# A new written order for the first phase of a linear-attention and MLP kernel

## The chip, the core and the metric

The kernel runs on one core of a Trainium2 chip. The metric is device microseconds (us) of one launch; lower is better. One execution of each kernel is also taken by the hardware profiler, and all rows below come from that one.

## The reference

Two parts run one after the other. The first is a gated linear recurrence over 768 time steps for 4 batches and 8 heads of size 48; the second is an MLP on the 3072 rows that come out of it, with a squared ReLU:

```
f = sigmoid(f_logit)
state = f[t] * state + outer(k[t], v[t])       # per batch and head, 48 x 48
y[t] = q[t] @ state
h = y.reshape(3072, 384) @ w_in                # 384 -> 2048
out = relu(h)**2 @ w_out                       # 2048 -> 384
```

All of it is float32.

## The kernel before

The sequence is cut into 6 blocks of 128 steps, and a block of all batches is 512 columns. In a block the 8 heads are worked in 4 units of two heads; units are numbered through, so that units 0 to 3 are block 0 and 4 to 7 block 1. The first three units of a block own the 128 rows of one tile x_0, x_1, x_2 each. The fourth has no rows of its own: the last 16 rows of each head are cut off the first three units' keys and queries (moved into `last_kq`), worked as unit 3 (or 7), written to `ys`, and moved from there into the rows left open in x_0, x_1 and x_2. Only then is the block's x whole and the MLP can begin on it.

The MLP is worked by 16 slices f of the 2048 hidden columns. A slice has an upward step (9 matmuls of 128x512 into `ph`), a square (three ScalarE passes, L195 to L197), a rest (one VectorE pass into `gl`, L202) and a downward step (9 matmuls into `po`). Each weight tile arrives as a raw tile of 384 KB and is decoded by ScalarE and VectorE into a high and a low float32 part, before a matmul can use it.

Two tables of short words, FIRST and SECOND, set the order of what is here called the first phase: units 0 to 7 and, for block 0, slices 0 to 5. Each word is a letter and a number, and emits its instructions on whatever engines it uses. TensorE, VectorE, ScalarE and SyncE run them in just that order. The words are:

- f, k, L: load of a unit's gates, keys and queries (L: 768 KB in one), v: of its values; i, o: raw tile of w_in or w_out.
- G: gates (ScalarE). K: scan and keys (VectorE L349, L355). Q: reciprocal, scan and queries (L361 to L366). T: transposes of the keys into `pk` (TensorE), N: their copy to `kn` (ScalarE). D: products with the values into `ds`; S: scores (TensorE). M: the mask (VectorE L441). C: the states (L456, L461). m: moves into `last_kq`; r, s: crossed copies (ScalarE L385, L393). Y: outputs into `py` (TensorE). H, X: high part (ScalarE L500) and low part (VectorE L504) of x. g: moves of `ys` into x (six transfers, L511).
- A, I, V, c, J decode a tile of w_in, B, O, Z, d, P one of w_out (ScalarE, VectorE, VectorE, ScalarE, VectorE; A and B are two ScalarE passes).
- U, R, E, W: upward step, square, rest and downward step of a slice. busy: filler transposes on TensorE whose result nothing reads.

So ScalarE's copies, VectorE's scans and the decoding of weights all stand in one order per engine, and what waits holds up all behind it. A raw tile's load is held by a marker: VectorE writes one element of the tile where the word stands, and SyncE's load has to follow that write. SyncE issues in its own order too, so loads behind a held one wait with it. GpSimd's order is not written; it issues m and g for blocks 0 and 1.

For units 4 to 7 `ds` and `py` share one PSUM buffer: D of a unit waits until X of the unit before it has read `py`, and Y waits until M and C have read `ds`.

After the first phase a loop of the remaining MLP slices runs, with the units of blocks 2 to 5 and the decoding of the other 20 weight tiles hooked in. Neither table touches it.

Of the kernel before, what the change touches and what calls it, by code (L numbers as in the profile page):

```python
# [15 lines left out]
I32 = mybir.dt.int32  # L16
# [8 lines left out]
HP = H // 2  # L25
# [8 lines left out]
NJ = DM // P  # L34
# [23 lines left out]
THIRD_AT, THIRD_OUT_AT = (11, 15, 18, 21), (15, 18, 21, 23)  # L58

FIRST = """  # L60
f0 k0 G0 v0 L1 K0 Q0 busy15 T0 v1 N0 busy2 D0 L2 r0 m0 S0 C0 G1 s0 K1 M0 busy5 T1 v2 Q1 Y0 N1 i0 o0
v3 L4 G2 D1 H0 m1 K2 S1 r1 X0 T2 A0 C1 v4 M1 s1 I0 N2 busy3 Y1 Q2 B0 D3 H1 V0 D2 m2 r2 X1 c0 S2 O0
i1 o1 L5 C2 Z0 s2 G4 M2 J0 d0 busy4 Y2 K4 r3 S3 H2 v5 C3 A1 T4 X2 M3 s3 Q4 N4 busy2 Y3 B1 H3 P0 m4
I1 i2 o2 L6 r4 X3 V1 g3 busy5 S4 G5 O1 c1 D4 K5 C4 v6 busy4 T5 A2 M4 s4 Z1 N5 busy5 Y4 Q5 d1
"""
SECOND = """
U0 H4 X4 r5 m5 i3 o3 v7 P1 J1 D5 R0 I2 U1 C5 G6 E0 s5 S5 V2 K6 R1 W0 c2 M5 T6 A3 E1 Y5 Q6 N6 W1 H5
i4 o4 i5 B2 X5 m6 J2 D6 r6 I3 U2 C6 B3 O2 s6 O3 S6 Z2 R2 Z3 M6 V3 Y6 r7 E2 d3 o5 H6 P3 d2 X6 c3 P2
S7 A5 J3 D7 M7 W2 C7 A4 I5 B4 I4 U3 V5 s7 V4 O4 c4 Z4 c5 Y7 J4 R3 J5 U4 H7 E3 B5 X7 U5 g7 d4 O5 R4
P4 Z5 W3 R5 E4 W4 d5 E5 P5 W5  # L70
"""


# [190 lines left out]
def fast_path(ctx, tc, moe, ident, low, fkqT, vN, w, out):  # L264
    nc = tc.nc
    V, G = nc.vector, nc.gpsimd
# [39 lines left out]
    class Unit:  # L306
# [23 lines left out]
        def load(self, *parts):  # L330
            if parts[0].start == 0:
                pool, bufs = (pro, 1) if self.t == NJ else (wk, NBUF)
                self.fkq = pool.tile([P, 3, NZ * CZ], F32, tag="fkq", name=f"fkq{self.nm}", bufs=bufs)
                self.ft, self.rr = self.fkq[:, 0, :NT], self.fkq[:, 0]
                self.view(self.fkq[:, 1:])
            for c in parts:
                nc.sync.dma_start(self.fkq[:, c, :NT], fkqT[self.blk, self.hp, :, c])

# [31 lines left out]
        def move(self):  # L370

            for h in range(2):
                r, at = h * C + D, h * C + self.hp * (C - D)
                (G if self.blk < 2 else nc.sync).dma_start(
                    *(t.rearrange("p a n -> p (a n)")[:, : NZ * CZ + NT] for t in (
                        last_kq[at : at + C - D], self.fkq[r : r + C - D, 1:]
                    ))
                )
# [127 lines left out]
        def parts(self):  # L506

            for j in range(NJ):
                for h in range(2):
                    r, at = h * C + D, h * C + j * (C - D)  # L510
                    (G if self.blk < 2 else nc.sync).dma_start(  # L511
                        self.x[j][r : r + C - D].bitcast(F32), self.x[NJ][at : at + C - D].bitcast(F32)
                    )

# [327 lines left out]
```

## Time and profile before

| | |
|---|---|
| median of 3 runs | 525.0 us (524.76 to 525.29) |
| the profiled execution's own time | 524.64 us |
| its span, first to last instruction | 522.9 us |
| PE busy | 495.7 us, 95% |
| DVE busy | 260.0 us, 50% |
| ACT busy | 284.3 us, 54% |
| mean granted TensorE clock | 0.967 of full speed |

PE is TensorE's matmuls, PEld its weight loads, DVE VectorE, ACT ScalarE, POOL GpSimd, SP SyncE. The 1.7 us outside the span are launch and end. A busy share over the whole span hides the first 90 us, where no engine is full. The granted clock is one of two levels, 1.2 GHz (shown as 0.50) or 2.4 GHz (1.00); a value between is a mean over a stretch.

### The profile page before, as it was taken

The numbers are of one execution on the slowest core, as the hardware profiler recorded it, in microseconds if no ns is written. First come the engines' busy times: TensorE is split into PE (matmuls) and PEld (weight loads), VectorE is DVE, ScalarE is ACT, GpSimd is POOL, SyncE is SP. The second block draws the span as 40 slices with busy tenths as digits, with TensorE's granted clock in tenths as the row PEclk, the third lists the DMA queues.
The fourth block names the chain that finished last, engine by engine and source line by source line (L and its number), as shares of the span: only waits on it lengthen the run. The fifth ranks groups of instructions, "written<-read, shape, count | busy, mean of one in ns | idle before, by whom it ended". The sixth has DMA issues, their size and how long they took to land.

```text
span 522.9 us, 11520 instructions
## 1 busy us (share of the span) xinstructions
PE 495.7 (95%) x4854; PEld 395.3 (76%) x4854; DVE 260.0 (50%) x487; ACT 284.3 (54%) x576; POOL 31.5 (6%) x73
## 2 busy tenths in 40 slices
PE   6787989999999999999999999999999999999994
PEld 5675767788787878777787777777777877788883
DVE  6795974998964454455254255244165332211111
ACT  3564886888756554455554546455546444444442
POOL 4231102000100000000000000000000000000000
PEclk9756989999999999999999999999999999999998
DMA  7657352366212204412004412003510001100001
GB/s 236 177 185 212 103 213 50 110 219 205 81 40 76 87 3 117 137 26 87 1 1 117 137 26 85 4 1 73 180 28 12 1 1 32 61 1 0 1 0 66
DMA packets 20236, 41.74 MB, mean 80 GB/s; under 512 B 2640, under 2 KB 5712, under 8 KB 20176
## 3 DMA queue, kind: packets, MB, share of 16 engines
q1 hardware_dynamic: 19408, 39.34, 24.9%
q0 software_dynamic: 768, 1.58, 1.4%
q8 instruction: 40, 0.66, 0.5%
q14 instruction: 20, 0.16, 0.1%
HBM read 31.46 MB, written 4.72 MB: 69 GB/s over the span
## 4 chain that ended last, share of the span: by engine, by line
PE 86%; DVE 4%; ACT 3%; DMA 3%; issue 1%; POOL 0%; DVEq 0%; POOLq 0%; ACTq 0%
PE po L211 38%; PE ph L185 37%; PE ds L423 3%; PE py L475 2%; PE ds L434 2%; PE py L487 2%; DMA x<-ys 2%; PE pk L399 2%; DVE gl L202 1%; ACT ph L196 1%; ACT ph L195 1%; DVE fkq L349 1%; DMA raw<-in_w_dram 1%; ACT gh L197 1%; DMA fkq<-in_fkqT_dram 1%
## 5 line engine op out<-in xcount | busy, mean ns | idle before, releaser
L185 PE MATMUL ph<-x,w 128*128 128x512 f32 x864 | 222.1, 402 | 6.0 <-DVE gl L202 3.1
L185 PEld LDWEIGHTS ph<-x,w 128*128 128x128 f32 x864 | 159.8, 189 | 46.7 <-DVE gl L202 5.8
L211 PE MATMUL po<-gh,w 128*128 128x512 f32 x576 | 181.6, 396 | 0.0
L202 DVE TENSOR_TENSOR gl<-ph,gh 128x512 fp32r<-128x512 f32 x96 | 66.3, 691 | 189.8 <-ACT gh L197 189.6
L195 ACT ACTIVATE ph<-ph 128x512 f32<-128x512 f32 x96 | 55.9, 582 | 148.4 <-PE ph L185 148.4
L211 PEld LDWEIGHTS po<-gh,w 128*128 128x128 f32 x576 | 108.5, 188 | 26.4
L211 PE MATMUL po<-gl,w 128*128 128x512 f32 x288 | 114.8, 398 | 0.0
L211 PEld LDWEIGHTS po<-gl,w 128*128 128x128 f32 x288 | 54.3, 188 | 13.4 <-issue 0.2
L197 ACT CAST gh<-ph 128x512 fp32r<-128x512 f32 x96 | 56.3, 586 | 3.0
L196 ACT ACTIVATE ph<-ph 128x512 f32<-128x512 f32 x96 | 55.9, 582 | 3.0
L475 PEld LDWEIGHTS py<-sc,vn 64*64 64x64 f32 (+1 forms) x768 | 24.3, 136 | 11.7 <-issue 9.8
L475 PE MATMUL py<-sc,vn 64*64 64x64 f32 (+1 forms) x768 | 28.4, 237 | 4.0 <-DVE sc L441 3.3
L354 POOL TENSOR_SCALAR fkq<-fkq 128x8 f32<-128x8 f32 x18 | 12.2, 678 | 323.2 <-DVE fkq L349 306.3
L487 PE MATMUL py<-rx,sx 48*48 48x64 f32 (+1 forms) x352 | 27.1, 225 | 1.1 <-ACT sx L393 1.0
L349 DVE TENSOR_TENSOR_SCAN fkq<-fz,dr 128x520 f32<-128x520 f32 x18 | 22.2, 1234 | 5.1 <-ACT fz L344 5.1
L487 PEld LDWEIGHTS py<-rx,sx 48*48 48x48 f32 (+1 forms) x352 | 23.0, 135 | 1.4 <-ACT sx L393 1.4
L130 ACT CAST w<-wa 128x384 fp32r<-128x384 f32 x32 | 16.2, 513 | 12.6 <-DVE wa L121 10.5
L363 DVE TENSOR_TENSOR_SCAN fkq<-fz,dz 128x520 f32<-128x520 f32 x18 | 22.3, 1241 | 0.6
L441 DVE TENSOR_TENSOR sc<-ds,mask 128x512 f32<-128x512 f32 x24 | 16.5, 688 | 10.5 <-PE ds L434 9.6
L500 ACT CAST x<-py 112x512 fp32r<-112x512 f32 x18 | 10.5, 585 | 18.8 <-PE py L487 18.8
L106 ACT ACTIVATE wa<-raw 128x384 f32<-128x384 f32 x32 | 17.6, 552 | 4.6 <-DMA raw<-in_w_dram 4.5
L487 PE MATMUL py<-fkq,sp 48*48 48x64 f32 (+1 forms) x264 | 19.7, 224 | 0.0
(76 smaller groups left out, 394.9 us busy)
## 6 DMA issues: line engine op xcount, KB each, us to landing
fkq<-in_fkqT_dram SPq DMA_DIRECT2D x17, 768.0 KB, 5.1
raw<-in_w_dram SPq DMA_DIRECT2D x32, 384.0 KB, 3.8
vn<-in_vN_dram SPq DMA_DIRECT2D x24, 192.0 KB, 4.8
out_dram<-ob SPq DMA_DIRECT2D x15, 256.0 KB, 2.1
last_kq<-fkq SPq DMA_DIRECT2D x24, 64.5 KB, 2.3
x<-ys SPq DMA_DIRECT2D x24, 64.0 KB, 2.3
last_kq<-fkq POOLq DMA_DIRECT2D x12, 64.5 KB, 4.1
x<-ys POOLq DMA_DIRECT2D x12, 64.0 KB, 3.7
```

The costliest lines, as they stand in the source:

```text
L106: nc.scalar.activation(a, upper_f, AF.Abs, scale=2.0**-112, accum_out=self.sums[:, 2 * f + i : 2 * f + i + 1])
L185: self.nc.tensor.matmul(self.ph[f], lhsT=l, rhs=r, start=j == 0 and i == 0, stop=j == NJ - 1 and i == 2)
L195: nc.scalar.activation(ph, ph, AF.Relu)
L196: nc.scalar.activation(ph, ph, AF.Square)
L197: nc.scalar.copy(out=gh, in_=ph)
L202: self.nc.vector.tensor_tensor(out=gl, in0=self.ph.pop(f), in1=gh.bitcast(F32), op=ALU.subtract)
L211: self.nc.tensor.matmul(self.po[e], lhsT=l, rhs=r, start=f == self.fs[0] and i == 0, stop=f == self.fs[-1] and i == 2,)
L349: V.tensor_tensor_scan(out=rr[:, ::-1], data0=self.fz[:, NZ * CZ : 0 : -1], data1=dr[:, ::-1], initial=0.0, op0=ALU.mult, op1=ALU.add,)
L363: V.tensor_tensor_scan(out=pp, data0=self.fz[:, : NZ * CZ], data1=dz, initial=0.0, op0=ALU.mult, op1=ALU.add)
L441: V.tensor_tensor(out=self.sc, in0=self.ds[:, :, B * D : B * (D + C)].rearrange("p h (b t) -> p h b t", t=C), in1=mask.unsqueeze(1).unsque ...
L475: nc.tensor.matmul(self.py[h * C : h * C + m, c, b * C : (b + 1) * C], lhsT=self.vn[rows, b, h * D : h * D + m], rhs=self.sc[rows, h, b], ...
L487: nc.tensor.matmul(self.py[h * C : h * C + m, c, b * C : (b + 1) * C], lhsT=s[rows, b * D : b * D + m], rhs=q[rows], start=False, stop=b = ...
```

## The change

Both tables are written anew: the same words for units and slices in another order, with 24 filler transposes in place of 45. Three edits come with it. The loads of units 2, 4, 5 and 6 get a marker like the weights have. The moves into `last_kq` of each block's third unit go from GpSimd to SyncE. Of the six moves of `ys` into x, the three of the first head half go to SyncE and three stay on GpSimd. One line of each table and the code:

```diff
 FIRST = """
-f0 k0 G0 v0 L1 K0 Q0 busy15 T0 v1 N0 busy2 D0 L2 r0 m0 S0 C0 G1 s0 K1 M0 busy5 T1 v2 Q1 Y0 N1 i0 o0
+f0 k0 v0 L1 G0 L2 K0 v1 Q0 busy11 T0 G1 N0 i0 K1 m0 r0 busy3 S0 o0 D0 G2 L4 v2 M0 T1 C0 K2 s0 N1 Y0
...
 SECOND = """
-U0 H4 X4 r5 m5 i3 o3 v7 P1 J1 D5 R0 I2 U1 C5 G6 E0 s5 S5 V2 K6 R1 W0 c2 M5 T6 A3 E1 Y5 Q6 N6 W1 H5
+U0 r4 M4 s4 O1 i4 Z1 A2 Y4 Q5 d1 U1 H4 o3 R0 X4 m5 P1 I2 D5 E0 R1 V2 S5 O2 W0 C5 r5 c2 E1 A3 Z2 W1
...
                 self.ft, self.rr = self.fkq[:, 0, :NT], self.fkq[:, 0]
                 self.view(self.fkq[:, 1:])
+                if 2 <= self.n < 2 * HP:
+                    V.memset(self.fkq.bitcast(I32)[0:1, 0, 0:1], 0)
             for c in parts:
...
-                (G if self.blk < 2 else nc.sync).dma_start(
+                (G if self.blk < 2 and self.hp < NJ - 1 else nc.sync).dma_start(
...
-                    (G if self.blk < 2 else nc.sync).dma_start(
+                    (G if self.blk < 2 and h else nc.sync).dma_start(
```

Three places show what the tables move. On ScalarE at the start of the program, before (`fz` are the gates, `kn` the copy of transposed keys, `rx` and `sx` crossed copies):

```order
L344 ACTIVATE fz_70<-fkq_0_130 128x8x64
L405 COPY kn_0_167<-pk_0_160 128x448
L407 COPY last_kn<-pk_0_160 128x8x16
L385 COPY rx_0_191<-fkq_0_130 48x256
L344 ACTIVATE fz_71<-fkq_1_136 128x8x64
L393 COPY sx_74<-sp_72 48x208
L405 COPY kn_1_261<-pk_1_226 128x448
```

And the same place in the changed kernel:

```order
L347 ACTIVATE fz_70<-fkq_0_130 128x8x64
L347 ACTIVATE fz_71<-fkq_1_135 128x8x64
L408 COPY kn_0_167<-pk_0_161 128x448
L410 COPY last_kn<-pk_0_161 128x8x16
L388 COPY rx_0_179<-fkq_0_130 48x256
L347 ACTIVATE fz_70<-fkq_2_138 128x8x64
L396 COPY sx_74<-sp_72 48x208
```

The gates of unit 1 now stand ahead of unit 0's key copy, and unit 2's gates ahead of the crossed copy `sx`.

On SyncE, the loads around the moves of block 0's x, before (`raw` are weight tiles, `fkq` and `vn` a unit's data); the six moves themselves are on GpSimd:

```order
L304 DMA raw_0_431<-in_w_dram 128x384
L304 DMA raw_1_434<-in_w_dram 128x384
L337 DMA fkq_1_437<-in_fkqT_dram 128x3x512
L341 DMA vn_1_501<-in_vN_dram 128x384
L304 DMA raw_0_559<-in_w_dram 128x384
L304 DMA raw_1_562<-in_w_dram 128x384
L337 DMA fkq_2_565<-in_fkqT_dram 128x3x512
```

And in the changed kernel (`x<-ys` are the moves, the other three stay on GpSimd):

```order
L304 DMA raw_1_487<-in_w_dram 128x384
L340 DMA fkq_2_506<-in_fkqT_dram 128x3x512
L304 DMA raw_0_537<-in_w_dram 128x384
L514 DMA x_0_115<-ys_3_548 16x1024
L514 DMA x_1_116<-ys_3_548 16x1024
L514 DMA x_2_117<-ys_3_548 16x1024
L344 DMA vn_1_620<-in_vN_dram 128x384
```

The load of unit 6 (`fkq_2`) is now queued ahead of the moves of x; before, SyncE issued it, with no marker, behind two weights and while GpSimd issued the moves. The values of unit 5 (`vn_1`) are now queued behind the moves; before, they were issued two weights earlier.

On TensorE around the first upward step (`ph_0`, of block 0's x), before; `py` are outputs of unit 4, `ds_1` the state products of unit 5:

```order
L487 MATMUL py_0_655<-rx_0_567,sx_74 48x64
L487 MATMUL py_0_655<-rx_0_567,sx_74 64x64
L185 MATMUL ph_0_703<-x_0_115,w_0_412 128x512 x3
L185 MATMUL ph_0_703<-x_1_116,w_0_412 128x512 x3
L185 MATMUL ph_0_703<-x_2_117,w_0_412 128x512 x3
L423 MATMUL ds_1_730<-vn_1_501,kn_1_647 64x48
L423 MATMUL ds_1_730<-vn_1_501,kn_1_647 48x48 x2
```

And in the changed kernel (`pw` are fillers, `ds_0` the scores of unit 4):

```order
L569 MATMUL pw<-ident 128x128 x6
L437 MATMUL ds_0_565<-fkq_0_221 64x64 x16
L185 MATMUL ph_0_642<-x_0_115,w_0_589 128x512 x3
L185 MATMUL ph_0_642<-x_1_116,w_0_589 128x512 x3
L185 MATMUL ph_0_642<-x_2_117,w_0_589 128x512 x3
L478 MATMUL py_0_667<-sc_0_655,vn_0_482 64x64
L478 MATMUL py_0_667<-sc_0_655,vn_0_482 48x64 x2
```

The first upward step now follows unit 4's scores, and unit 4's outputs come behind it instead of ahead of it.

## Rows read from the trace of the kernel before

**Rows 1.** Busy time by stretch: us, PE, PEld, DVE, ACT, POOL, PEclk, DMA share, GB/s

```profile
10.79:36.67 25.88, 17.93 (x411) 15.66 (x410) 22.00 (x44) 14.16 (x36) 5.74 (x12) 0.69 0.54 162
36.67:50.30 13.63, 10.43 (x154) 7.96 (x157) 9.54 (x20) 5.58 (x13) 4.50 (x11) 0.63 0.92 249
50.30:86.70 36.40, 33.68 (x488) 26.90 (x489) 27.06 (x56) 28.70 (x64) 4.86 (x10) 0.94 0.41 126
86.70:100.00 13.30, 12.28 (x52) 9.26 (x52) 10.10 (x26) 10.74 (x26) 0.00 (x0) 1.00 0.34 102
100.00:520.00 420.00, 413.67 (x3667) 328.87 (x3665) 185.42 (x331) 220.94 (x431) 11.53 (x24) 1.00 0.20 60
```

**Rows 2.** Chain that ended last, 38 to 87 us: start, us, what

```profile
38.38 8.89 DMA x<-ys
47.40 2.90 PE ph L185 x6
...
86.70 2.12 PE ph L185 x9
```

**Rows 3.** VectorE in order of time: start, us, what, [idle before it and releaser]

```profile
35.98 0.68 DVE L504 TENSOR_TENSOR ys<-py,ys 112x512 fp32r<-112x512 f32 x1
...
40.25 0.36 DVE L456 TENSOR_TENSOR sp<-state,fkq 112x192 f32<-112x192 f32 x1
...
40.91 0.68 DVE L441 TENSOR_TENSOR sc<-ds,mask 128x512 f32<-128x512 f32 x1
41.51 0.55 DVE L117 SCALAR_TENSOR_TENSOR wa<-raw,wa 128x384 int32<-128x384 int32 x1
41.98 0.20 DVE L361 RECIPROCAL dz<-fkq 128x8 f32<-128x8 f32 x1
42.21 1.24 DVE L363 TENSOR_TENSOR_SCAN fkq<-fz,dz 128x520 f32<-128x520 f32 x1
43.49 0.69 DVE L366 TENSOR_TENSOR fkq<-fkq 128x512 f32<-128x512 f32 x1
44.10 0.68 DVE L504 TENSOR_TENSOR x<-py,x 112x512 fp32r<-112x512 f32 x1
44.72 0.55 DVE L132 TENSOR_TENSOR w<-wa,w 128x384 fp32r<-128x384 f32 x1
...
45.19 0.55 DVE L132 TENSOR_TENSOR w<-wa,w 128x384 fp32r<-128x384 f32 x1
...
51.40 0.35 DVE L461 TENSOR_TENSOR state<-sp,ds 112x192 f32<-112x192 f32 x1 [4.92 <-PE ds L423]
```

**Rows 4.** DMA issues from 36.05 to 39.9 us: size, median us to landing

```profile
fkq<-in_fkqT_dram SPq DMA_DIRECT2D x1, 768.0 KB, 10.2
x<-ys POOLq DMA_DIRECT2D x6, 64.0 KB, 7.9
```

**Rows 5.** ScalarE in order of time, 7 to 10 us

```profile
7.48 0.53 ACT L405 COPY kn<-pk 128x448 f32<-128x448 f32 x1 [3.21 <-PE pk L399]
...
9.85 0.63 ACT L344 ACTIVATE fz<-fkq 128x512 f32<-128x512 f32 x1 [0.80 <-DMA fkq<-in_fkqT_dram]
```

**Rows 6.** DMA issues from 15.3 to 18 us

```profile
raw<-in_w_dram SPq DMA_DIRECT2D x2, 384.0 KB, 4.4
```

**Rows 7.** TensorE in order of time, 36 to 40 us, at the half clock

```profile
36.72 1.13 PE L434 MATMUL ds<-fkq 48*64 48x64 f32 x32 [0.33 <-DVE ys L504]
37.62 1.05 PE L423 MATMUL ds<-vn,kn 64*64 64x48 f32 x32
38.60 1.11 PE L566 MATMUL pw<-ident 128*128 128x128 f32 x4
```

**Rows 8.** DMA issues from 77 to 82 us

```profile
x<-ys POOLq DMA_DIRECT2D x6, 64.0 KB, 2.2
```

**Rows 9.** The stretch 50.30 to 86.70 us, instructions on py alone: us, PE, PEld, DVE, ACT

```profile
50.30:86.70 36.40, 3.49 (x192) 3.07 (x192) 2.06 (x3) 1.76 (x3) 0.94 0.41 126
```

More of the change, by code (lines that the diff above doesn't have):

```diff
@@ L60 @@
 FIRST = """
-f0 k0 G0 v0 L1 K0 Q0 busy15 T0 v1 N0 busy2 D0 L2 r0 m0 S0 C0 G1 s0 K1 M0 busy5 T1 v2 Q1 Y0 N1 i0 o0
-v3 L4 G2 D1 H0 m1 K2 S1 r1 X0 T2 A0 C1 v4 M1 s1 I0 N2 busy3 Y1 Q2 B0 D3 H1 V0 D2 m2 r2 X1 c0 S2 O0
-i1 o1 L5 C2 Z0 s2 G4 M2 J0 d0 busy4 Y2 K4 r3 S3 H2 v5 C3 A1 T4 X2 M3 s3 Q4 N4 busy2 Y3 B1 H3 P0 m4
-I1 i2 o2 L6 r4 X3 V1 g3 busy5 S4 G5 O1 c1 D4 K5 C4 v6 busy4 T5 A2 M4 s4 Z1 N5 busy5 Y4 Q5 d1
+f0 k0 v0 L1 G0 L2 K0 v1 Q0 busy11 T0 G1 N0 i0 K1 m0 r0 busy3 S0 o0 D0 G2 L4 v2 M0 T1 C0 K2 s0 N1 Y0
+B0 Q1 D1 H0 v3 i1 A0 L5 T2 X0 m1 S1 r1 Q2 N2 G4 D2 A1 C1 m2 S2 M1 s1 r2 Y1 C2 K4 s2 G5 D3 H1 M2 r3
+S3 X1 o2 I1 Y2 v4 C3 V1 o1 s3 I0 c1 T4 H2 M3 N4 X2 L6 J1 busy2 Y3 i2 O0 B2 K5 H3 X3 busy2 T5 V0 g3
+D4 Z0 Q4 N5 c0 d0 J0 m4 busy6 S4 G6 P0 v5 B1 C4 i3
 """
 SECOND = """
-U0 H4 X4 r5 m5 i3 o3 v7 P1 J1 D5 R0 I2 U1 C5 G6 E0 s5 S5 V2 K6 R1 W0 c2 M5 T6 A3 E1 Y5 Q6 N6 W1 H5
-i4 o4 i5 B2 X5 m6 J2 D6 r6 I3 U2 C6 B3 O2 s6 O3 S6 Z2 R2 Z3 M6 V3 Y6 r7 E2 d3 o5 H6 P3 d2 X6 c3 P2
-S7 A5 J3 D7 M7 W2 C7 A4 I5 B4 I4 U3 V5 s7 V4 O4 c4 Z4 c5 Y7 J4 R3 J5 U4 H7 E3 B5 X7 U5 g7 d4 O5 R4
-P4 Z5 W3 R5 E4 W4 d5 E5 P5 W5
+U0 r4 M4 s4 O1 i4 Z1 A2 Y4 Q5 d1 U1 H4 o3 R0 X4 m5 P1 I2 D5 E0 R1 V2 S5 O2 W0 C5 r5 c2 E1 A3 Z2 W1
+M5 d2 I3 s5 v6 P2 V3 A4 Y5 J2 K6 i5 c3 U2 H5 B3 X5 o4 J3 T6 R2 Q6 U3 o5 N6 O3 m6 r6 D6 E2 R3 S6 Z3
+v7 W2 C6 d3 M6 s6 P3 r7 Y6 E3 A5 I4 W3 V4 H6 I5 c4 X6 B4 J4 S7 V5 D7 M7 B5 U4 C7 c5 O5 s7 Z5 R4 Y7
+J5 O4 Z4 U5 H7 E4 d4 X7 d5 P4 g7 P5 R5 W4 E5 W5
 """
```

## The prediction

> **What bounds the kernel now.** I read the busy time by stretch first, then the chain of waits, then each engine in order of time, last the DMA issues with their time to landing. From 100 to 520 us TensorE is busy 413.67 of 420 us at a granted clock of 1.00 [rows 1]; the tables don't reach in there, so that part keeps its length. What is saved before comes off the end one for one. The first phase ends at 86.70 us, where block 1's first upward step starts [rows 2].
>
> In the first phase no engine is full. From 10.79 us, the first scan of unit 1, to 36.67 us, the end of X3, VectorE is nearest to it: 22.00 of 25.88 us, with TensorE's clock at 0.69 on average. From 36.67 to 50.30 us nearly nothing goes on but DMA: a share of 0.92 at 249 GB/s, the clock at 0.63. From 50.30 to 86.70 us TensorE is busy 33.68 of 36.40 us at 0.94 [rows 1]. The middle stretch is one wait in the chain: X3 starts at 35.98 us [rows 3], then GpSimd issues the moves of ys into x, 8.89 us go by until one has landed, and the upward step's last six matmuls run from 47.40 to 50.30 us [rows 2]. VectorE stands still for 4.92 us of it, waiting for products of unit 5 that are queued on TensorE behind that step [rows 3]. The moves took 7.9 us to land, because the 768 KB load of unit 6, which itself took 10.2 us, was issued among them [rows 4].
>
> **Up to the first scan of unit 1: no gain.** In before, ScalarE copied unit 0's keys at 7.48 us and did unit 1's gates at 9.85 us, when their load had landed [rows 5]. Now the gates stand ahead of that copy. The load has the same bytes ahead of it, so I leave its landing at 9.8 us; the key copy slips to 10.5 us, and with it products and state of unit 0 (C0). This costs VectorE nothing, because the state now stands behind the scan, which starts at 10.5 us (10.79 in before). If the load lands later for company, all slips with it.
>
> **From there to the end of X3.** What an operation costs on VectorE is read from one start to the next, where they follow without a gap [rows 3]: scan 1.28, product behind it 0.61, reciprocal 0.23, mask 0.60, a state's two operations 0.66, low part of x 0.62, any operation of a decode 0.47. The new order has between K1 and X3 six scans (7.68), six products (3.66), two reciprocals (0.46), four masks (2.40), four states (2.64), four low parts (2.48) and five decode operations (2.35): 21.7 us. From 10.5 us that is 32.2 without a wait. Followed step by step over the engines, the low parts have to wait for their high parts on ScalarE, since Y at the half clock ends late: 0.3, 0.5, 0.85 and 0.25 us, 1.9 in all. X3 ends at **34.1 us**. Bounds: no wait (32.2) and the 3.9 us in before, 25.88 less 22.00 (36.1).
>
> What has to stay hidden here are loads. The unit loads with a marker go out at 2.9, 12.4, 17.7 and 30.5 us and their gates are wanted at 12.2, 20.1, 24.5 and 36.6: 6 to 9 us each, where a load of this size took 10.2 at worst [rows 4]. The first weight of w_out is read ahead of unit 0's high part on ScalarE. Its marker now stands behind K1, at 12.4 us; with the 4.4 us of such loads [rows 6] it is there by 16.8, and I count the first 0.3 us of waiting for it. This cover is thin: what lands 1 us later moves X3 by about as much. The first weight of w_in gains: it goes out behind Q0, at 8.6 us. The moves into `last_kq` that SyncE now issues wait for Q2 (20.7 us) and are wanted by unit 3's scores at 26; behind them on SyncE is a weight whose marker comes at 26.2 in any case, so they hold up nothing.
>
> **From X3 to the end of the first upward step.** TensorE transposes unit 5's keys until about 34.6 us, then products of unit 4 (0.98), six fillers (0.25 each) and scores (0.90), by the half-clock rows [rows 7]. Scores need Q4: on VectorE two decode operations and Q4 (0.94 and 2.12) end at 37.2, so the scores end at 38.1 us. The upward step of nine matmuls at 2.90/6 us [rows 2] ends at **42.5 us**; at full clock (2.12 us for nine, last row of rows 2) it would be 40.2. Has x landed? At 34.1 us two loads are on their way, unit 6's (768 KB, issued at about 30.5) and a weight (384 KB). At 249 GB/s, 0.28 MB of their 1.18 are left; with the six moves (0.39) and unit 5's values behind them on SyncE (0.20; wanted only by products at 46 us) this takes 3.5 us, and with the 2.2 us of a move by itself [rows 8] all is there by 39.8. The third tile is read at 41.0. So the wait is gone, and what is late next is TensorE's own row of products, fillers and scores. If the moves are as late as before, counted from X3 (13.6 us to the end of the step), the step ends at 47.7.
>
> The Trainium skill, "DMA: Bandwidth & Descriptors", section "Issuing engines are not separate DMA queues", says that transfers issued from several engines run on the same 16 DMA engines and interleave, so that the split saves issue time alone. The trace agrees in that the moves took 7.9 us beside loads and 2.2 without; by that rule alone the second engine brings the landing nothing.
>
> **From there to the end of the phase.** The same work as in before's stretch from 50.30 us, and one Y more, since unit 4's outputs now come behind the step: 3.49/3 = 1.16 us [rows 9]. TensorE's busy time is then 33.68 + 1.16 = 34.8 us at before's clock; at the full clock 0.06 x 33.68 = 2.0 less. Its idle time was 2.7 us. VectorE and ScalarE, with 27.06 and 28.70 us in before [rows 1], get none less, so all three are near full, and each waits for the others. I take half of before's idle time, 1.4, since VectorE is no longer 4.9 us behind at the start. Sum: 42.5 + 34.8 + 1.4 = **78.7 us**. Bounds: full clock and no idle time, 75.3; clock and idle as before, 80.0.
>
> **Behind it.** Block 1's x moves end with no load beside them, 2.2 us [rows 8], under the last two downward steps (4.2). The six raw weights that SyncE issued long before now stand behind its three moves, until about 75 us; the first is wanted by ScalarE behind the copies of po at 79.3, 4.4 us later, which is just the landing time [rows 6]. I count nothing; if it lands like the slowest load (10.2, rows 4), ScalarE's squares wait 5.8 us, and so does TensorE, less the two steps it has in hand (4.2). Fewer fillers cost nothing where the half clock is already counted.
>
> **The sum.** 86.7 - 78.7 = 8.0 us off 524.64, the profiled execution's own time: 516.6. The median of the runs shown lies 0.36 above that execution; I give 516.7.
>
> **Rivals.**
> 1. *x lands as late as before.* For it: the moves share the queues with 1.2 MB of loads. Against: those go out 3 to 4 us ahead of the moves, not among them. The step ends at 47.7 and the phase at 83.9: 2.8 us gained, 521.8. The skill's rule above would give this if nothing but the second engine were to help.
> 2. *The clock comes back early.* TensorE has work without a pause from 33.5 us on; if the step runs at 2.4 GHz (2.2 us) and nothing falls back (2.0), the phase ends at 74.5: 512.4. Against: in before the clock was low still at 50 us, and VectorE allows little more.
> 3. *Slower: the held loads come too late on ScalarE.* The decodes' first passes stand ahead of the high parts of x and the key copies, and their loads go out only when VectorE reaches the marker. The first w_out weight and the second w_in weight each have 4 to 5 us. Should both need the 10.2 us of the slowest load [rows 4], each costs about 6 us, X3 ends at 46 and the phase at 91: 529. It decides from 8.0 us of such waits. Against: few bytes are on their way at 12 and 18 us, and two weights landed in 4.4 us beside a unit's load.
> 4. *The gain is given back in the loop*, by the six weights behind the moves and slips of 0.5 us at many places: no change, 524.6.
>
> **How the numbers follow.** My forecast (513.5 to 519.5) has 0.55, x late (519.5 to 523.6) 0.20, the clock 0.12, slower 0.08, no change 0.05. A difference of under 0.2%, about 1 us, can't be told from none here. Faster is 0.55 + 0.20 + 0.12 = 0.87, same 0.05, slower 0.08. The range 512.5 to 522.0 leaves out part of the clock case, the end of x late, and the last two: some 0.2.
>
> **What would show it.** In the changed kernel: X3 on VectorE ends near 34 us; the first upward step runs without a wait for x from 38 to 42.5 us; block 1's first upward step begins near 78.7 us; from there on the same length as before. It is wrong if that first step waits for x<-ys, if ScalarE waits for raw weights over 2 us in all, or if the part behind the first phase is over 1 us longer than 436.2 us (522.9 - 86.7).

## The result and the profile after

The changed kernel takes 518.73 us (median of 4 runs, 517.66 to 520.02) where the kernel before took 524.88 (4 runs) on the same chip: a ratio of 0.9889, 95% interval 0.9856 to 0.9921. It is faster, by 1.1%, as forecast, and 2.0 us over the 516.7 predicted. The profiled execution took 519.51 us, its span 517.8.

The busy time by stretch, to be laid beside [rows 1]. The stretches have the same bounds in the work: first scan of unit 1, end of X3, end of the first upward step, block 1's first upward step. Columns as there.

```profile
9.64:34.96 25.32, 17.55 (x443) 15.41 (x437) 21.73 (x44) 14.45 (x36) 6.42 (x11) 0.73 0.67 201
34.96:45.04 10.08, 6.57 (x86) 4.68 (x87) 8.94 (x20) 6.35 (x16) 3.94 (x8) 0.70 0.82 232
45.04:81.28 36.24, 33.94 (x551) 26.12 (x552) 28.65 (x59) 28.45 (x63) 2.92 (x6) 0.99 0.30 77
```

Against before, the first stretch is 0.56 us shorter and begins 1.15 us earlier; the second is 10.08 us instead of 13.63; the third is 36.24 where it was 36.40. So of the 5.3 us that separate the two first upward steps' ends (50.30 and 45.04), 1.7 lie ahead of X3's end and 3.55 behind it, and nothing was gained later: from 81.28 us to the end of the span it is 436.5 us, where it was 436.2 behind 86.70.

The chain that ended last (start, us, what) shows the places, and answers to [rows 2]:

```profile
19.69 7.21 DMA last_kq<-fkq
...
32.40 1.25 DVE fkq L352
33.86 0.60 POOL fkq L357
34.54 1.40 POOL low L357
35.93 4.68 DMA x<-ys
40.62 0.25 issue
40.86 4.18 PE ph L185 x9
```

The moves of x are still in the chain, with 4.68 us instead of 8.89. Two things stand ahead of them whose time I had not counted: the landing of the moves into `last_kq` that SyncE now issues, and two small operations of GpSimd.

TensorE and VectorE in order of time (columns as in [rows 3]) around the first upward step:

```profile
38.06 0.69 PE L437 MATMUL ds<-fkq 48*64 48x64 f32 x32 [1.41 <-DVE fkq L369]
40.86 4.18 PE L185 MATMUL ph<-x,w 128*128 128x512 f32 x9 [2.10 <-DMA x<-ys]
```

```profile
34.28 0.68 DVE L507 TENSOR_TENSOR ys<-py,ys 112x512 fp32r<-112x512 f32 x1
...
47.23 0.69 DVE L507 TENSOR_TENSOR x<-py,x 112x512 fp32r<-112x512 f32 x1 [2.99 <-ACT x L503]
```

X3, the first VectorE row, begins at 34.28 us and ends at 34.96. The scores are through at 38.75, then TensorE waits 2.10 us for x and runs all nine matmuls in 4.18 us. VectorE's wait did not go either: it is 2.99 us at unit 4's low part, whose outputs now stand behind the step, where it was 4.92 in [rows 3].

The windows of the same time give the clock (last three columns: PEclk, DMA share, GB/s; the first figure behind the length is PE):

```profile
34.00:36.00 2.00, 1.38 (x38) 1.19 (x39) 2.00 (x5) 0.02 (x1) 1.92 (x3) 1.00 0.98 313
36.00:38.00 2.00, 0.66 (x6) 0.42 (x4) 1.93 (x4) 2.00 (x5) 1.44 (x3) 1.00 0.99 319
38.00:40.00 2.00, 0.69 (x32) 0.56 (x32) 1.86 (x6) 1.49 (x5) 0.96 (x2) 0.77 0.96 203
40.00:42.00 2.00, 1.14 (x3) 0.98 (x4) 1.93 (x7) 1.91 (x7) 0.00 (x0) 0.50 0.59 91
```

The clock is full up to 38 us and falls to 0.50 between 38 and 40. TensorE was busy only 0.66 and 0.69 of 2 us in the two windows from 36 to 40: it had waited 1.41 us for VectorE ahead of the scores, and behind them it waited for x.

### The profile page after: what moved, and what is told of

Read it like the earlier page. It is cut to its first block, busy times and chain, and to the rows that moved or that the text cites. A ratio compares the mean times of both kernels' runs of the same rounds, so it can differ in the third digit from the quotient of the medians.

```text
span 517.8 us, 11474 instructions
## 1 busy us (share of the span) xinstructions
PE 489.5 (95%) x4833; PEld 389.0 (75%) x4833; DVE 260.2 (50%) x491; ACT 283.9 (55%) x576; POOL 29.2 (6%) x63
## 4 chain that ended last, share of the span: by engine, by line
PE 81%; DVE 6%; DMA 5%; ACT 4%; issue 2%; SPq 1%; POOL 0%; DVEq 0%; ACTq 0%; POOLq 0%
PE ph L185 36%; PE po L211 36%; DMA last_kq<-fkq 2%; PE ds L437 2%; PE py L478 2%; PE ds L426 2%; PE py L490 2%; PE pk L402 1%; DMA fkq<-in_fkqT_dram 1%; DVE gl L202 1%; DVE fkq L352 1%; ACT ph L196 1%; ACT ph L195 1%; ACT gh L197 1%; DMA x<-ys 1%
## 5 line engine op out<-in xcount | busy, mean ns | idle before, releaser
L503 ACT CAST x<-py 112x512 fp32r<-112x512 f32 x18 | 10.5, 583 | 19.7 <-PE py L490 19.7
```

## The experiments

All times below are medians, each ratio against the kernel before in the same series (524.02 to 524.48 us there). One table carries the readings that recur, from one profiled execution each: end of the first upward step (U0), start of block 1's first upward step (as the order of time has it: 86.54 in before, where the chain has 86.70), the difference, and what is left of the span behind that.

| kernel | median us | ratio, 95% | U0 ends | block 1 starts | between | behind |
|---|---|---|---|---|---|---|
| before | 524.88 | 1 | 50.30 | 86.54 | 36.2 | 436.4 |
| changed | 518.73 | 0.9889 (0.9856, 0.9921) | 45.04 | 81.28 | 36.2 | 436.5 |
| e0 changed again | 518.73 | 0.9885 (0.9856, 0.9913) | 45.74 | 82.25 | 36.5 | 436.4 |
| e1 all moves on GpSimd | 519.89 | 0.9915 (0.9896, 0.9933) | 45.97 | 82.93 | 37.0 | 436.5 |
| e2 old order, new issuers | 528.75 | 1.0088 (1.0069, 1.0106) | 52.44 | 90.77 | 38.3 | 436.2 |
| e3 fillers in the wait | 516.67 | 0.9873 (0.9852, 0.9895) | 42.43 | 78.36 | 35.9 | 436.2 |
| e4 old order, quiet moves | 524.83 | 1.0018 (0.9997, 1.0040) | 46.30 | 89.09 | 42.8 | 436.5 |
| e5 no load markers | 517.33 | 0.9882 (0.9859, 0.9904) | 42.24 | 79.01 | 36.8 | 436.5 |
| e6 weight behind the moves | 514.60 | 0.9845 (0.9815, 0.9875) | 40.70 | 76.71 | 36.0 | 436.2 |
| e8 loads beside the moves | 521.56 | 0.9962 (0.9945, 0.9978) | 47.62 | 84.00 | 36.4 | 436.0 |
| e9 weight behind, fillers | 516.16 | 0.9846 (0.9825, 0.9868) | 42.22 | 78.20 | 36.0 | 436.3 |
| e10 the same, no markers | 514.80 | 0.9810 (0.9792, 0.9828) | 40.08 | 76.87 | 36.8 | 436.4 |
| e11 old order, three loads earlier | 520.32 | 0.9925 (0.9907, 0.9942) | 44.80 | 81.80 | 37.0 | 436.4 |

The last column never moves by more than 0.5 us, whatever was done to the tables.

### Which part of the change pays: the issuers?

**e0_changed_again**: the changed kernel, unaltered.

> The changed kernel as it is, to stand beside the next three on the same chip. 517.5 to 520.0 us; the first phase (start of block 1's first upward step) ends at 81.0 to 81.6 us of its profile, the first upward step waits some 2 us for the moves of x and runs at the half clock (4.2 us).

The median was the same, but the profiled execution differs in one thing. DMA issues from 30 to 46 us: size, median us to landing. First the changed kernel's profile above (30 to 37 us), with the weight issued at 32.38 us and SyncE's first move, at 34.99, by themselves below:

```profile
x<-ys SPq DMA_DIRECT2D x3, 64.0 KB, 4.7
x<-ys POOLq DMA_DIRECT2D x3, 64.0 KB, 4.5
...
raw<-in_w_dram SPq DMA_DIRECT2D x1, 384.0 KB, 6.7
...
x<-ys SPq DMA_DIRECT2D x1, 64.0 KB, 4.9
```

And e0's, the weight issued at 31.44 us and the first move at 34.05:

```profile
x<-ys SPq DMA_DIRECT2D x3, 64.0 KB, 6.3
x<-ys POOLq DMA_DIRECT2D x3, 64.0 KB, 6.3
...
raw<-in_w_dram SPq DMA_DIRECT2D x1, 384.0 KB, 9.1
...
x<-ys SPq DMA_DIRECT2D x1, 64.0 KB, 6.7
```

X3 came 0.94 us earlier in e0 (33.34), the moves landed 1.6 us slower, and U0 waited 3.74 us for x. The same instructions thus differ by over a microsecond in the very term in dispute; differences of about that size between two single profiles prove nothing below.

The rows also say where the difference sits. The weight ahead of the moves landed at 39.0 us in the one profile and at 40.5 in the other, and the first move of SyncE right behind it, at 39.9 and 40.7. It is so in every profile that records the landing of the load ahead of SyncE's first move (after, e0, e2, e3, e5, e8, e9, e10): that move landed 0.2 to 1.5 us behind the load. So what varies is less the moves than the loads in front of them.

**e1_moves_on_gpsimd**: both issuer edits undone.

```diff
-                (G if self.blk < 2 and self.hp < NJ - 1 else nc.sync).dma_start(
+                (G if self.blk < 2 else nc.sync).dma_start(
...
-                    (G if self.blk < 2 and h else nc.sync).dma_start(
+                    (G if self.blk < 2 else nc.sync).dma_start(
```

> The new tables and markers, but all moves into last_kq and all six moves of x back on GpSimd. Theory (the order of steps and loads makes the gain): the move of unit 2 no longer stands behind unit 5's load on SyncE and lands about 2 us earlier, so X3 ends near 34 us; the six issues take 2.9 us in place of 1.8, so x is whole about 1.5 us later after X3: within 1 us of the changed kernel, 517.5 to 520. Rival (the second issuer makes the gain): at least half of the 6 us is lost, 521.5 or more.

Measured 0.9915: about 1 us lost, and the intervals of e0 and e1 overlap. The order alone, with its markers, keeps three quarters of the gain (0.85% of 1.15%).

**e2_old_order_new_issuers**: the kernel before, with those two edits the other way.

> The old tables without markers, but the moves on SyncE and GpSimd as in the changed kernel. Theory (the order makes the gain): the loads still run beside the moves, and SyncE's half now even stands behind them; no gain above 1 us, 523.8 to 526. Rival (the second issuer makes it): 521.5 or less, the first upward step ends 3 us earlier after X3.

Slower, by 0.9%, and beyond the 526 us that I had allowed. Its DMA issues from 36 to 40.5 us:

```profile
raw<-in_w_dram SPq DMA_DIRECT2D x2, 384.0 KB, 4.6
fkq<-in_fkqT_dram SPq DMA_DIRECT2D x1, 768.0 KB, 10.3
x<-ys POOLq DMA_DIRECT2D x3, 64.0 KB, 8.3
x<-ys SPq DMA_DIRECT2D x3, 64.0 KB, 9.8
```

In the old order SyncE has two weights and unit 6's load to issue first (36.60 to 38.19 us), so its half of the moves goes out at 38.28 us and takes 9.8 us to land. So the second issuer costs time where its row has loads to issue ahead of the moves; that it gains where it has none is not shown, since e1's 1 us is not clear of noise.

### Or the loads around the moves?

**e8_loads_back_beside_moves**: the changed kernel with unit 6's load and the weight issued directly ahead of SyncE's moves, much as they were issued beside the moves before.

```diff
-... N4 X2 L6 J1 busy2 Y3 i2 O0 B2 K5 H3 X3 busy2 T5 V0 g3
+... N4 X2 J1 busy2 Y3 O0 B2 K5 H3 X3 L6 i2 busy2 T5 V0 g3
```

> The changed kernel with unit 6's load and that weight issued directly ahead of the moves of x, behind X3, about as in the kernel before. Theory (the loads among the moves make x late): the moves land 7 us or more after their issue, the first upward step starts at 42.5 us or later and everything behind it slips by 2 to 3 us: 520.5 to 523; a part of this is that unit 6's gates wait on ScalarE for the later load. Rival: the step starts as in the changed kernel (40.9 to 41.6), 518 to 520.

The upward step in TensorE's order of time:

```profile
43.44 4.18 PE L185 MATMUL ph<-x,w 128*128 128x512 f32 x9 [5.74 <-DMA x<-ys]
```

This one edit gave back two thirds of the gain (0.9962 left of 0.9885). SyncE's moves took 7.8 us to land, much as the 7.9 of [rows 4], and TensorE waited 5.74 us for them, instead of 2.10 or 3.74. The stretch behind is 36.4 us, unmoved.

**e11_old_order_loads_earlier**: the kernel before, with nothing moved but three loads.

```diff
-... busy4 Y2 K4 r3 S3 H2 v5 C3 A1 T4 X2 M3 s3 Q4 N4 busy2 Y3 B1 H3 P0 m4
-I1 i2 o2 L6 r4 X3 V1 g3 busy5 S4 G5 O1 ...
+... busy4 Y2 K4 i2 o2 L6 r3 S3 H2 v5 C3 A1 T4 X2 M3 s3 Q4 N4 busy2 Y3 B1 H3 P0 m4
+I1 r4 X3 V1 g3 busy5 S4 G5 O1 ...
```

> The kernel before with nothing changed but the place of three loads: two weights and unit 6's data are issued at about 30 us, 6 us ahead of the moves of x, in place of beside them; no decode moves. Theory (the wait for x, made by loads beside the moves, is what the old order paid and the new one saved): the first upward step starts at 42.9 us right behind unit 4's outputs and ends by 46; block 1 starts 3.5 to 4.5 us earlier, 519.5 to 521.5, most of what the change gained. Rival (the old order loses the same time behind that step, since VectorE's and ScalarE's lists bind there): the step ends by 46 and block 1 starts within 1 us of before, 523 to 525.

Ratio 0.9925. The loads go out between 30.0 and 32.2 us; X3 stays about where it was (35.59 us, 35.98 in before), the moves take 3.8 us to land, and the upward step stands right behind unit 4's outputs at the full clock. TensorE in order of time:

```profile
42.24 0.27 PE L487 MATMUL py<-rx,sx 48*48 48x64 f32 x2
42.44 2.36 PE L185 MATMUL ph<-x,w 128*128 128x512 f32 x9
```

U0 ends at 44.80, where the whole new order with its new issuers had 45.04. Three words moved in the old table give two thirds of the change's gain (0.75% of 1.11%). With e8 this is shown from both sides: the old order paid for loads issued beside the moves.

**e4_old_order_quiet_moves**: a first try at the same, which missed. Unit 6's load no longer stands behind two weights and goes out at 26.90 us, but those weights and unit 6's values were held until behind Q5.

```diff
-I1 i2 o2 L6 r4 X3 V1 g3 busy5 S4 G5 O1 c1 D4 K5 C4 v6 busy4 T5 A2 M4 s4 Z1 N5 busy5 Y4 Q5 d1
+I1 L6 r4 X3 V1 g3 busy5 S4 G5 O1 c1 D4 K5 C4 busy4 T5 M4 s4 Z1 N5 busy5 Y4 Q5 i2 o2 v6 d1
-... D5 R0 I2 U1 ...
+... D5 R0 A2 I2 U1 ...
```

> The kernel before (old tables, moves on GpSimd), but no load is issued beside the moves of x: unit 6's load stands ahead of X3, two weights and unit 6's values come only behind Q5, and the first weight's decode that needs one of them moves behind the first square. Theory (the loads among the moves make x late): the moves land in 2.2 to 3.5 us in place of 7.9, the first upward step starts at about 42.9 us, right behind unit 4's outputs, and ends by 45.5 to 47 us (50.3 before); 520 to 522 us. Rival (the moves are slow by themselves or by GpSimd's issue): the step ends at 49 us or later, 523.5 to 526.

The moves landed in 2.3 us and U0 ended 4.0 us earlier than before, as expected; but the time was that of before, since the stretch behind became 42.8 us. VectorE in order of time:

```profile
50.11 0.56 DVE L111 SCALAR_TENSOR_TENSOR wa<-wa,raw 128x384 int32<-128x384 int32 x1 [3.25 <-ACT raw L108]
```

VectorE waits 3.25 us for ScalarE's pass over the weight that was now late, with unit 5's state and low parts behind it in its row. That wait is in size half of the 6.6 us lost; the rest I did not trace. As a test of the loads this run is confounded, and e11 took its place: a load must be moved ahead of the moves, and not merely away from them.

### The half clock and the markers

**e3_fillers_in_the_wait**: more filler transposes around unit 4's scores.

```diff
-D4 Z0 Q4 N5 c0 d0 J0 m4 busy6 S4 G6 P0 v5 B1 C4 i3
+D4 Z0 Q4 N5 c0 d0 J0 m4 busy16 S4 busy18 G6 P0 v5 B1 C4 i3
```

> The changed kernel with 10 more filler transposes ahead of unit 4's scores and 18 behind them, so that TensorE works through the two stretches in which it stood still ahead of the first upward step (1.4 and 2.1 us). Theory (the half clock of that step comes from TensorE standing still while x is awaited): the granted clock stays 1.00 to the step, the step takes 2.1 to 2.6 us in place of 4.2 and unit 4's outputs 1.1 in place of 1.5; phase end 1.5 to 2.5 us earlier, 515.5 to 517.5. Rival (the clock falls here whatever TensorE does, as in the kernel before, where fillers stood and the clock was 0.50): no gain, 518 to 520.

The windows of e3:

```profile
36.00:38.00 2.00, 1.84 (x44) 1.53 (x43) 1.97 (x5) 1.67 (x4) 0.86 (x3) 1.00 0.68 165
38.00:40.00 2.00, 2.00 (x18) 1.76 (x17) 1.83 (x7) 1.94 (x6) 0.65 (x2) 1.00 0.67 165
40.00:42.00 2.00, 1.90 (x9) 1.61 (x9) 1.93 (x6) 1.95 (x6) 0.00 (x0) 1.00 0.68 191
```

With TensorE at work 1.84 and 2.00 of 2 us the clock stays at 1.00, and the step's nine matmuls take 2.33 us instead of 4.18. That the half clock came from TensorE standing still ahead of the step is thereby shown; its price is 1.85 us in the step. Fillers stand in both stretches here, so e3 does not tell the 1.41 us ahead of the scores from the 2.10 us for x; e9 below bears on that. The medians differ by 2.1 us, but x also landed in 4.0 us here, and the intervals overlap (0.9873 and 0.9885).

**e5_no_load_markers**: the markers of the unit loads left out.

```diff
-                if 2 <= self.n < 2 * HP:
+                if False:
```

> The changed kernel without the markers on the loads of units 2, 4, 5 and 6. Theory (order, not markers): unit 4's and 5's loads stand behind weights that have markers of their own and keep their place; unit 6's goes out at about 30.2 in place of 31.7 us, and x can land by up to 1.5 us earlier; 517 to 519.5. Rival (holding the loads matters): 520.5 or more, with an earlier load in the way of a weight or a move.

0.9882: the same as the changed kernel, whose markers thus gain nothing. X3 came at 32.62 us, U0 waited 1.27 us for x.

### A better version

**e6_weight_behind_moves**: the raw weight that SyncE issued 2.6 us ahead of the moves now goes behind them.

```diff
-... J1 busy2 Y3 i2 O0 B2 K5 H3 X3 busy2 T5 V0 g3
+... J1 busy2 Y3 O0 B2 K5 H3 X3 busy2 T5 V0 g3 i2
```

> The changed kernel with the weight that SyncE issued 2.6 us ahead of the moves of x (i2, 384 KB) issued behind them. Theory (x waits for what is queued ahead of it): x lands some 1.2 us earlier after X3 and the first upward step starts as much earlier; the weight's first decode pass on ScalarE then waits up to 1 us; 517 to 518.5. Rival (the landing of moves is set by their own number or by chance, 4.0 to 6.3 us in three profiles of the same order): no change, 518 to 520.

514.60 us, more gained than I expected. Five of its six runs, 513.86 to 515.13, are below all of e0's (515.20 at the least), the sixth took 518.53; the intervals of the two ratios still overlap (0.9815 to 0.9875, and 0.9856 to 0.9913). DMA issues from 30 to 46 us:

```profile
x<-ys SPq DMA_DIRECT2D x3, 64.0 KB, 2.6
x<-ys POOLq DMA_DIRECT2D x3, 64.0 KB, 3.5
```

The moves landed in 2.6 and 3.5 us. In order of time the step had no wait, though part of it still ran at the half clock:

```profile
37.01 3.69 PE L185 MATMUL ph<-x,w 128*128 128x512 f32 x9
```

**e9_weight_behind_and_fillers**: e6, with 16 fillers ahead of the scores and 3 behind (`busy16 S4 busy3` for `busy6 S4`).

> The changed kernel with both edits that helped: the weight issued behind the moves of x, and fillers in the stretches where TensorE stood still (10 more ahead of unit 4's scores, 3 behind them). Theory (the late x and the half clock are two costs): the first upward step starts near 37.3 us at the full clock and takes 2.3 us in place of 3.7; 1 to 2 us below the kernel with the weight moved alone, 512.5 to 514. Rival (they are one cost, and VectorE's list binds behind it): 514 to 515.5, no better than that one.

No better than e6, 0.9846 against 0.9845, and at 516.16 us above what the theory and its rival had allowed. The step ran in 2.32 us, but x took 5.2 us to land in this execution and was waited for: unit 6's load ahead of it, issued at 30.64 us, took 8.3. TensorE in order of time, and a window of 2 us ahead of the step:

```profile
39.90 2.32 PE L185 MATMUL ph<-x,w 128*128 128x512 f32 x9 [1.69 <-DMA x<-ys]
```

```profile
38.00:40.00 2.00, 0.32 (x3) 0.14 (x2) 1.83 (x6) 0.96 (x2) 0.50 (x2) 1.00 0.96 283
```

e6's profile has x on time and a low clock, e9's the reverse, so this pair leaves open whether the two costs add up. It does show that a wait of 1.69 us for x need not bring the half clock with it. In the changed kernel and in e5, where the fillers ahead of the scores are six and TensorE also waited 1.4 us there, the clock fell; here, with sixteen, it stayed at 1.00. This rests on one profile each.

**e10_and_no_load_markers**: e9 and e5 together.

> As the last, and without the markers on the unit loads. Theory (unit 6's load goes out 1.5 us earlier, and x has nothing ahead of it in any case): no difference, 512.5 to 514.5. Rival (earlier loads clear the queues further): 0.5 to 1 us less.

The upward step in TensorE's order of time:

```profile
37.74 2.34 PE L185 MATMUL ph<-x,w 128*128 128x512 f32 x9
```

514.80 us (513.80 to 515.04), the lowest ratio, 0.9810: 1.9% below the kernel before, and by the two ratios 0.75% below the changed kernel, which did not run in that series. In its profile there is neither a wait for x nor the half clock, and U0 ends at 40.08 us. What of e10's lead over e9 is due to the missing markers is not settled: their intervals meet at 0.9825.

## Why the prediction was right, and where its sizes were off

**Where the gain lies: right.** The first upward step came 5.3 us earlier, the profiled pair's spans differ by 5.1, and both the stretch behind it and the rest of the program kept their length. e8 and e11 show the cause that the prediction named: unit 6's load and the weights are no longer issued among the moves. They still run beside them (DMA share 0.98 and 0.99 from 34 to 38 us), which is where the prediction's sizes failed, below. One reading of the old kernel was too strong: from 36.67 to 50.30 us not "nearly nothing goes on but DMA", for [rows 1] has TensorE busy 10.43 and VectorE 9.54 of 13.63 us; what holds is that the chain there is the wait for x. And the sum's last step was left out: 516.6 and the 0.36 that it names make 517.0, not 516.7.

**First scan of unit 1, put at 10.5 us: it came 0.86 earlier.** Unit 1's load landed earlier than I left it (gates at 8.98 us), so the scan began at 9.64.

**X3's end, put at 34.1 us: it came 0.86 later, with 1.7 us more in the stretch than counted.** The earlier start hid half of that, which is luck. VectorE's work was the 21.7 us of the sum (21.73). Its idle time was 3.6 us instead of 1.9, near the upper bound of 3.9, and in other places: of the four low parts that were to wait, only one did, and the largest waits stand ahead of states. Three of its waits, in order of time:

```profile
21.90 0.36 DVE L459 TENSOR_TENSOR sp<-ds,fkq 112x192 f32<-112x192 f32 x1 [1.01 <-PE ds L437]
...
26.46 0.69 DVE L507 TENSOR_TENSOR x<-py,x 112x512 fp32r<-112x512 f32 x1 [0.89 <-ACT x L503]
...
28.54 0.36 DVE L459 TENSOR_TENSOR sp<-ds,last_kq 112x192 f32<-112x192 f32 x1 [0.91 <-PE ds L437]
```

And ScalarE's waits for loads in the same stretch, in order of time:

```profile
15.04 0.55 ACT L106 ACTIVATE wa<-raw 128x384 f32<-128x384 f32 x1 [1.28 <-DMA raw<-in_w_dram]
...
21.70 0.55 ACT L106 ACTIVATE wa<-raw 128x384 f32<-128x384 f32 x1 [1.82 <-DMA raw<-in_w_dram]
...
25.33 0.63 ACT L347 ACTIVATE fz<-fkq 128x512 f32<-128x512 f32 x1 [1.50 <-DMA fkq<-in_fkqT_dram]
```

The loads were not hidden. Unit 5's was issued at 17.50 us and its gates waited 1.50 us for it; the high part for which VectorE waits 0.89 us at 26.46 stands behind them. And the moves of unit 2 into `last_kq` held up nothing behind them on SyncE, as I wrote, but I had not costed their own landing: 7.21 us from 19.69, beside that same load, to 26.91, where the scores were wanted at 26. The state of unit 3, the last VectorE row, waits for the scores behind those. In e1 these moves were on GpSimd, and X3 came no earlier than in e0 (33.42 and 33.34), so the issuer itself isn't to blame. Which share of the 1.7 us each of these waits holds, no run separates.

**x landed by 39.8 us, the third tile read at 41.0: the step that failed.** What failed is "so the wait is gone", and with it one of the prediction's own signs: the step waited 2.10 us for x. I let it begin at 38.1 us, on a first tile that I had not timed, and checked only the third. The landing was mis-sized too. At X3's end only 0.28 MB of the two loads were to be left; in the trace they were issued at 31.67 and 32.38 us and landed at 37.1 and 39.0, the second 4.1 us behind X3's end, and the moves behind them, from 39.9 to 41.4. So all six were there 6.4 us after X3's end where 5.7 were counted, nearer than the parts of that sum deserve. Nor do the tiles come far apart: each has a piece on either queue, and GpSimd's pieces went out only from 35.93 us, the first landing at 40.61. GpSimd in order of time:

```profile
33.86 0.59 POOL L357 TENSOR_SCALAR fkq<-fkq 128x8 f32<-128x8 f32 x1 [8.93 <-DVE fkq L352]
34.54 1.45 POOL L357 TENSOR_SCALAR low<-fkq 128x8 f32<-128x8 f32 x1
35.93 1.51 POOL L514 DMA_DIRECT2D x<-ys  x3
```

So the first matmul was held to within 0.8 us of the last landing, and the nine ran from 40.86 to 45.04 instead of 38.1 to 42.5: 2.5 us late, of which 0.86 is X3 and about 1.7 this. I had taken the first rival for a matter of landing as late as before; in truth a part of it came true, a wait of 2.1 us (3.7 in e0) at a landing nearly halved. e6 shows the same cause: with the second of the two loads issued behind the moves the wait was gone.

**The half clock in that step: right in the number, in part by luck.** 4.18 us were measured where 4.35 were counted. But I had carried the half clock on from before, for the products, fillers and scores as well. In the trace the clock was full from 34 to 38 us, as rival 2 had it, the scores took 0.69 us and not 0.90, and it fell only ahead of the step, because rival 2's work without a pause was not there. e3 shows what it takes: work for TensorE in the stretches where it stood still.

**The stretch behind: right as a length, by offsetting errors.** 36.2 us predicted, 36.24 measured, but with the clock at 0.99 (0.94 in before) and TensorE busy 33.94, not 34.8, and 2.3 us idle instead of 1.4. The length was 35.9 to 36.5 us in seven of the kernels in the table; as it is the same at a clock of 0.94 and of 0.99, TensorE alone does not set it.

**Rivals 3 and 4: small parts of both.** ScalarE at the weight that stands behind block 1's moves, in order of time:

```profile
82.93 0.55 ACT L106 ACTIVATE wa<-raw 128x384 f32<-128x384 f32 x1 [0.86 <-DMA raw<-in_w_dram]
```

With the two above and one of 0.35 us at 32.30, ScalarE waits 4.3 us in all for raw weights up to there. I had written that over 2 us would speak against the forecast, and the bound was passed, the second of the three signs. It was set in the wrong place: what counts is how much of a wait reaches VectorE, and rival 3's delay of X3 to 46 us stayed far off. Behind the last of them, at 82.93, the rest of the program still took its 436.5 us, so the third sign, over 1 us more than 436.2, did not show.

**The two issuers.** The prediction drew on the Trainium skill, "DMA: Bandwidth & Descriptors", section "Issuing engines are not separate DMA queues": the split saves issue time alone. The runs agree as far as they can tell: e1 loses 1 us of 6, not clear of noise, and in the profiles the step begins at 41.79 us in e1 and 41.56 in e0, from X3 at 33.42 and 33.34. e2 adds that the place in the issuer's own row decides.

**Open.** Why the same weight, ahead of the same moves, lands in 6.7 us in one execution and 9.1 in the next. It limits how finely the remaining terms can be told apart.

## What to carry to other kernels

When a small transfer stands in the chain, look at which loads were queued ahead of it and beside it, and when they land, before looking at who issues it: moving three loads in the old table gave two thirds of what the new one gave. A second issuer gained at most 1 us here, not clear of noise, and cost 0.9% where its row had loads to issue first. When a tile is put together from several transfers, cost the wait by the last piece of its first tile. And give TensorE work in the stretches ahead of such a step, since the half clock there was a second price, of 1.85 us.

## What the runs showed of the hardware that was not expected

- The six moves of 64 KB landed in 2.3 us (e4, where unit 6's load had landed 2.2 us before the first went out), 2.6 and 3.5 us (e6), 3.8 (e11), and 8.3 and 9.8 us (e2), and in 4.7 or 6.3 us in two executions of one and the same program. Where a load stood ahead of it on SyncE and its landing is recorded, SyncE's first move landed 0.2 to 1.5 us behind that load, in all eight profiles.
- TensorE's clock stayed full over a wait of 1.69 us in e9, and fell to 0.50 in the changed kernel in a wait of 2.10 us, ahead of which stood one of 1.41 and 0.69 us of work.
- GpSimd's operation on 128x8 (`low`) took 1.45 us at 34.54 and 1.24 us at 14.95, where it took 0.23 in all six units of the first phase before. Both slow ones ended within 0.2 us of the end of VectorE's scan or decode beside them; whether that is the reason wasn't tried.
- A load's time to landing did not follow from its bytes alone: unit 6's 768 KB landed in 5.4 us in the changed kernel, 7.5 in e0 and 10.2 in [rows 4].
